# Causal mask of a linear-attention kernel: a DVE product against an ACT copy and a select on Pool

## The chip, the cores and the metric

One Trainium2 chip, one core. The metric is the device time of one execution in microseconds (us); the kernel before takes 953.3 us (median of three runs, 953.12 to 953.48). TensorE is called PE here (its weight loads PEld), VectorE DVE, ScalarE ACT, GpSimd Pool, and SyncE, which issues the transfers, SP.

## What is computed

Gated linear attention over 4 batches x 8 heads x 768 positions of width 48, its output normalised and passed through two feed-forward blocks on 3072 tokens of width 384.

```python
f = 1.0 / (1.0 + np.exp(-f_logit))
for t in range(S):
    state = f[:, :, t, :, None] * state + np.einsum('bhd,bhe->bhde', k[:, :, t], v[:, :, t])
    y[:, :, t] = np.einsum('bhd,bhde->bhe', q[:, :, t], state)
...
rms = np.sqrt(np.mean(x * x, axis=-1, keepdims=True) + 1e-06)
xn = x / rms * rms_g
g = xn @ w_gate
silu = g * (1.0 / (1.0 + np.exp(-g)))
x = silu * (xn @ w_val) @ w_out          # 384 -> 1536 -> 384
...
r = np.maximum(x @ w_in, 0.0)
out = (r * r) @ w_out                    # 384 -> 2048 -> 384
```

## The kernel before

The recurrence is cut into chunks of 128 positions. A unit is one chunk of one batch; there are 24 units, in 6 groups of 4 (512 tokens). For each unit DVE scans the gates (scan_b, scan_a), scales k and q by the decays (mul_k, mul_q), PE forms the 128x128 scores of the 8 heads (`scores`, lines 320 to 329) in two PSUM tiles of 128x512, one for each half of the heads, and the scores are made causal by `mask_part` (lines 331 to 334), called twice for a unit by `masked`. Before the change this is one DVE product of a PSUM tile with a 0/1 tile, written to an SBUF tile `sm`. `attend` (line 355) then multiplies `sm` with v and adds the state's part, giving y; `kv` and `state_add` move the state on; `norm`, `power` (on Pool), `norm2`, `xtrans`, `xhigh`, `xlow` turn y into the transposed input of the feed-forward blocks, split in a high and a low part so that three fast matmuls stand for one in full precision.

The tile `sm` comes from a ring of four buffers (tag "sm", `bufs=4`). The same ring serves `x3o` (`evac_x3_part`, line 806), the three 128x512 tiles in which the first feed-forward block's result of a group is copied out of PSUM by ACT and stored to memory. So the second `sm` tile of the first unit after a group's end waits until a store of `x3o` has landed.

The order on every engine is written out by hand, and each engine works through its own queue in that order:

- Units 0 to 7 and the first group's feed-forward block follow the list FIRST (lines 32 to 48): ma and mb are the two halves of the mask, sc the scores, y attend, kv the state's product, gr, gf the gates, kc the copy of k, no, nr the norm, xh, xl the two splits, ws, wb, wc, wh, wz the conversion of the first block's weights (ws and wh on ACT, wb, wc and wz on DVE), G, V, O the matmuls of one hidden feature block, si, vs, hh, hl the work on their results. G0 is the first of these matmuls.
- Groups 1 to 5 run in steps (`phase1`, line 888). A group has 36 steps, step s = 36 x group + 3 x feature block + 0, 1 or 2. PE does G in the first of three, V in the second, O of the block before in the third; ACT's silu stands in the first, DVE's vs and ACT's hh in the second, DVE's hl in the third. The accumulators g and v have one PSUM bank each, so the next G cannot begin before silu has read the last one. In a step (`segment`, line 794) the planned side work of that step comes first, then silu, vs, hh or hl, then the planned PE work of the attention.
- `plan_unit` (line 670) puts a unit's parts at fixed steps: scores at the end of step s, kcopy and masked in step s + 1, attend at the end of step s + 2, norm in s + 3.
- All other side work is the preparation of the second block's weights, done once, spread over groups 1 to 5: load a raw pair, scale (ACT), three bit operations (DVE), sums and differences (DVE), splits in a high and a low part (ACT and DVE), each split stored to memory; then `open` (line 762), which opens new pools and begins fetching the first 8 of the prepared tiles of 384 KB (`fetch_part`, line 920); then x3, which loads the second block's input (`x3_load`, line 941), and the splits of this input (`x_split`, line 985), an ACT cast and a DVE subtraction for each.
- A planner places these jobs (lines 777 to 784). It goes through them in one order, and a job's step is the first that is not before the step of the job ahead of it and not before its own earliest step (so many steps after a named job: 1 after the last split for `open`, 3 after x3 for the first x split), and in which the job's estimated cost still fits under 2.1 us on each engine it uses, plus an allowance for steps with PE work of the attention. What the units take of each step is entered first from the table COST (lines 687 to 691), the pair (DVE, ACT). The estimates are constants of the code.

After step 215 comes the second feed-forward block (`phase2`, line 1158), which holds no mask.

Of the kernel before, what the change touches and what calls it, by code (L numbers as in the profile page):

```python
# [13 lines left out]
ALU = mybir.AluOpType  # L14
PSUM = bass.MemoryType.PSUM

P = 128
B, H, S, D = 4, 8, 768, 48
C = 128
# [170 lines left out]
def tile_linear_attention_moe(  # L190
# [11 lines left out]
    nc = tc.nc  # L202
# [23 lines left out]
    mask = cp.tile([P, C], F32, name="mask")  # L226
# [29 lines left out]
    U = {}  # L256
# [73 lines left out]

    def mask_part(u, hf):
        sm = ap_.tile([P, 4, C], F32, tag="sm", name=f"sm{u}_{hf}", bufs=4)
        nc.vector.tensor_mul(sm, U[u]["sc", hf], mask.unsqueeze(1).broadcast_to([P, 4, C]))
        U[u]["sm", hf] = sm

    def masked(u):
        mask_part(u, 0)
        mask_part(u, 1)
# [345 lines left out]
    for gi in range(1, NU - 1):  # L684
        for j in range(UG):
            plan_unit((gi + 1) * UG + j, gi * NG + (3 if gi == 1 and j == 0 else (1, 10, 19, 28)[j]))
    COST = dict(
        scan_b=(1.4, 0), keep_end=(0, 0.2), scan_a=(1.2, 0), mul_k=(0.7, 0), mul_q=(0.7, 0), masked=(1.4, 0),
        kcopy=(0, 0.6), gate=(0, 2.2), decay=(0, 1.5), norm=(0, 1.0), norm2=(0, 0.6), state_add=(0.7, 0),
        xhigh=(0, 1.1), xlow=(1.05, 0),  # L690
    )
# [144 lines left out]
    def piece(kind, i):  # L836
        if kind in ("lr", "lk", "lf", "lq", "lv"):
            load_part(kind[1], i)
        elif kind in ("gr", "gf"):
            gate(i) if i >= UG else gate_part(kind[1], i)  # L840
        elif kind in ("ma", "mb"):
            mask_part(i, kind == "mb")
        elif kind in unit_piece:
            unit_piece[kind](i)
        elif kind in pair_piece:
            pair_piece[kind](w1_order[i])
        else:
            step_piece(kind, 0, i)
# [476 lines left out]
```

## Time and profile before

| | us |
|---|---|
| median of three runs | 953.3 |
| the profiled execution | 954.61 |
| its span, first to last instruction | 952.9 |

| engine | busy us | share of the span |
|---|---|---|
| PE | 928.7 | 97% |
| DVE | 629.4 | 66% |
| ACT | 496.3 | 52% |
| Pool | 17.8 | 2% |

How to read it: the table is an average over stages that have different limits. Matmul ends are modelled, so the start of a matmul to the start of the next says more than its busy time. In a timeline row the columns are the start and the duration in us, the engine, the line, the operation, the tile written and those read, the shape and the count; a bracket tells how long the engine stood idle before it and what ended that.

### The profile page before, as it was taken

What the parts mean: (1) busy time and instruction counts of PE and PEld (TensorE: products, weight loads), DVE (VectorE), ACT (ScalarE), POOL (GpSimd) and SP (SyncE); (2) the same over time, 40 slices, a digit from 0 to 9 for tenths busy, and PEclk for the clock granted to TensorE, in tenths of its full rate; (3) what the DMA queues carried; (4) which work ended last, traced back from release to release, by engine and by line L of the source; (5) the groups of instructions that cost most, each with busy time, mean ns of one, the idle gap of its engine ahead of it and who ended that gap; (6) DMA issues with size and microseconds to landing.
All of it is one profiled execution on the core that took longest, in us unless ns stands there. A gap on an engine that the chain in (4) does not pass through costs nothing.

```text
span 952.9 us, 15645 instructions
## 1 busy us (share of the span) xinstructions
PE 928.7 (97%) x6025; PEld 822.2 (86%) x6025; DVE 629.4 (66%) x1147; ACT 496.3 (52%) x1056; POOL 17.8 (2%) x42
## 2 busy tenths in 40 slices
PE   6899999999999999999999999999999999999996
PEld 4687877888888888888888889999999999999996
DVE  7999957655665676666663736756775676666552
ACT  4877555445454555455543425556546554645541
POOL 1000000000000000000000000000000000000000
PEclk6899999999999999999999999999999999999999
DMA  9356342335245154064236057540754075315300
GB/s 336 146 197 223 137 152 88 120 120 194 77 169 183 73 199 160 36 234 155 89 111 248 2 198 256 192 146 12 240 161 129 18 228 164 123 34 182 109 25 28
DMA packets 58081, 135.67 MB, mean 142 GB/s; under 512 B 6800, under 2 KB 25232, under 8 KB 58000
## 3 DMA queue, kind: packets, MB, share of 16 engines
q1 hardware_dynamic: 58000, 134.61, 41.5%
q8 instruction: 49, 0.80, 0.3%
q14 instruction: 32, 0.26, 0.1%
HBM read 108.63 MB, written 25.95 MB: 141 GB/s over the span
## 4 chain that ended last, share of the span: by engine, by line
PE 88%; DVE 4%; DMA 3%; ACT 2%; issue 1%; SPq 0%; POOL 0%; DVEq 0%; ACTq 0%
PE o L644 7%; PE o L643 7%; PE o L642 7%; PE X L1001 7%; PE Y L1001 5%; PE v L642 5%; PE acc L642 5%; PE v L644 5%; PE v L643 5%; PE acc L644 5%; PE acc L643 5%; PE g L642 4%; PE g L643 4%; PE g L644 4%; PE sc L326 2%; PE T L1001 2%
## 5 line engine op out<-in xcount | busy, mean ns | idle before, releaser
L644 PE MATMUL o<-wb,h 128*128 128x384 f32 x384 | 128.6, 335 | 0.0
L643 PE MATMUL o<-wb,h 128*128 128x384 f32 x384 | 128.3, 334 | 0.0
L642 PE MATMUL o<-wb,h 128*128 128x384 f32 x384 | 128.3, 334 | 0.0
L868 DVE TENSOR_TENSOR sg<-v,sg 128x512 f32<-128x512 f32 x72 | 49.6, 689 | 90.9 <-PE v L644 86.4
L871 ACT CAST hh<-sg 128x512 fp32r<-128x512 f32 x72 | 44.4, 617 | 99.4 <-DVE sg L868 99.4
L863 ACT ACTIVATE sg<-g 128x512 f32<-128x512 f32 x72 | 43.0, 597 | 84.7 <-PE g L644 84.6
L1001 PE MATMUL X<-xc,wa 128*128 128x384 f32 x360 | 82.5, 336 | 0.0
L644 PEld LDWEIGHTS o<-wb,h 128*128 128x128 f32 x384 | 72.1, 188 | 0.5
L642 PEld LDWEIGHTS o<-wb,h 128*128 128x128 f32 x384 | 72.1, 188 | 0.0
L643 PEld LDWEIGHTS o<-wb,h 128*128 128x128 f32 x384 | 72.1, 188 | 0.0
L1001 PE MATMUL Y<-xc,wa 128*128 128x384 f32 x300 | 68.3, 335 | 0.0
L1001 PEld LDWEIGHTS X<-xc,wa 128*128 128x128 f32 x360 | 63.8, 188 | 1.8 <-ACT d L1076 1.2
L1080 DVE TENSOR_TENSOR c<-T,c 128x384 f32<-128x384 f32 x40 | 22.3, 558 | 52.7 <-PE T L1001 43.6
L1001 PEld LDWEIGHTS Y<-xc,wa 128*128 128x128 f32 x300 | 53.3, 188 | 0.7 <-DVE c L1080 0.6
L873 DVE TENSOR_TENSOR hl<-sg,hh 128x512 fp32r<-128x512 f32 x72 | 48.9, 681 | 6.0 <-ACT hh L871 5.8
L1031 DVE TENSOR_TENSOR h<-d,h 128x384 fp32r<-128x384 f32 x60 | 32.9, 554 | 26.2 <-ACT h L1030 25.9
L1030 ACT CAST h<-d 128x384 fp32r<-128x384 f32 x60 | 30.2, 511 | 34.4 <-PE o L644 34.4
L1076 ACT COPY d<-X 128x384 f32<-128x384 f32 x40 | 19.2, 480 | 54.7 <-PE X L1001 54.7
L642 PE MATMUL v<-xh,wh_v 128*128 128x512 f32 x108 | 44.2, 410 | 0.0
L642 PE MATMUL g<-xh,wh_g 128*128 128x512 f32 x108 | 43.3, 401 | 0.9 <-ACT xh L443 0.9
L642 PE MATMUL v<-xh,wh_g 128*128 128x512 f32 x108 | 43.7, 405 | 0.0
L642 PE MATMUL acc<-hh,wh_o 128*128 128x512 f32 x108 | 43.2, 400 | 0.0
(181 smaller groups left out, 2243.7 us busy)
## 6 DMA issues: line engine op xcount, KB each, us to landing
wa<-w2d_c SPq DMA_DIRECT2D x100, 384.0 KB, 3.5
raw<-in_w_dram SPq DMA_DIRECT2D x18, 768.0 KB, 4.3
ff<-in_ff_dram SPq DMA_DIRECT2D x20, 516.0 KB, 4.8
qk<-in_qk_dram SPq DMA_DIRECT2D x20, 512.0 KB, 5.7
w2d_c<-ws_c SPq DMA_DIRECT2D x50, 192.0 KB, 2.0
raw_a<-in_w_dram SPq DMA_DIRECT2D x22, 384.0 KB, 3.8
wb<-w2d_b SPq DMA_DIRECT2D x16, 384.0 KB, 3.9
v<-in_vp_dram SPq DMA_DIRECT2D x24, 192.0 KB, 5.7
```

The source lines that it names most:

```text
L642: nc.tensor.matmul(o, lh, rh, start=first, stop=False)
L643: nc.tensor.matmul(o, lh, rl, start=False, stop=False)
L644: nc.tensor.matmul(o, ll, rh, start=False, stop=last)
L863: nc.scalar.activation(dd["s", f], dd["g", f], AF.Silu)
L868: nc.vector.tensor_mul(dd["s", f], dd["v", f], dd["s", f])
L871: nc.scalar.copy(dd["h", f][0], dd["s", f])
L873: nc.vector.tensor_sub(dd["h", f][1], dd["s", f], dd["h", f][0].bitcast(F32))
L1001: nc.tensor.matmul(o, w[a], x[:, b], start=first and n == 0, stop=last and n == 2, skip_group_check=True,)
L1030: nc.scalar.copy(t[:, 0], r)
L1031: later(lambda: nc.vector.tensor_sub(t[:, 1], r, t[:, 0].bitcast(F32)))
L1076: nc.scalar.copy(t, bk[b])
L1080: nc.vector.tensor_add(t, bk[b], t)
```

## The change

`mask_part` no longer multiplies on DVE. ACT copies the score tile from PSUM to `sm`, and Pool then zeroes, in place, the entries on the wrong side of the diagonal, in all four heads of the tile at once. The planner's entry for masked moves from 1.4 us of DVE to 1.2 us of ACT. Nothing else is edited; the places of ma, mb and masked in the orders stay.

```diff
     def mask_part(u, hf):
         sm = ap_.tile([P, 4, C], F32, tag="sm", name=f"sm{u}_{hf}", bufs=4)
-        nc.vector.tensor_mul(sm, U[u]["sc", hf], mask.unsqueeze(1).broadcast_to([P, 4, C]))
+        nc.scalar.copy(sm, U[u]["sc", hf])
+        nc.gpsimd.affine_select(
+            out=sm, in_=sm, compare_op=ALU.is_ge, fill=0.0,
+            base=-(C - 1), pattern=[[0, 4], [1, C]], channel_multiplier=1,
+        )
         U[u]["sm", hf] = sm
...
     COST = dict(
-        scan_b=(1.4, 0), keep_end=(0, 0.2), scan_a=(1.2, 0), mul_k=(0.7, 0), mul_q=(0.7, 0), masked=(1.4, 0),
+        scan_b=(1.4, 0), keep_end=(0, 0.2), scan_a=(1.2, 0), mul_k=(0.7, 0), mul_q=(0.7, 0), masked=(0, 1.2),
         kcopy=(0, 0.6), gate=(0, 2.2), decay=(0, 1.5), norm=(0, 1.0), norm2=(0, 0.6), state_add=(0.7, 0),
```

## Rows read from the trace of the kernel before

**Rows 1.** The page, part 1: busy us, share and instructions of each engine.

```profile
PE 928.7 (97%) x6025; PEld 822.2 (86%) x6025; DVE 629.4 (66%) x1147; ACT 496.3 (52%) x1056; POOL 17.8 (2%) x42
```

**Rows 2.** Busy time by stage; last columns: granted PE clock, DMA share, GB/s.

```profile
24.50:36.30 11.80, 7.34 (x127) 6.05 (x127) 11.66 (x21) 11.39 (x30) 1.98 (x3) 0.93 0.35 137
36.30:145.00 108.70, 105.19 (x729) 83.96 (x731) 96.26 (x146) 71.49 (x137) 2.34 (x4) 0.97 0.50 177
145.00:500.00 355.00, 354.75 (x2576) 292.18 (x2574) 230.94 (x431) 180.56 (x396) 9.20 (x16) 1.00 0.38 133
500.00:545.00 45.00, 45.00 (x200) 37.14 (x200) 22.39 (x42) 16.29 (x32) 0.00 (x0) 1.00 0.37 132
...
519.00:521.00 2.00, 2.00 (x10) 1.66 (x9) 0.12 (x1) 0.43 (x1) 0.00 (x0) 1.00 1.04 409
```

**Rows 3.** Instructions of line 333, ns shortest/median/longest; then what it waited for.

```profile
L333 DVE TENSOR_TENSOR sm<-sc,mask x32: 679/681/692, 145.8 to 482.5; 128x512 f32<-128x512 f32 x32
...
  DMA x3d<-x3o: 10.3, 3
```

**Rows 4.** Timeline of ACT: a PSUM copy of 128x512 and its follower.

```profile
16.46 0.59 ACT L352 COPY ktok<-ktp 128x512 f32<-128x512 f32 x1
16.95 0.63 ACT L289 ACTIVATE r<-r 128x512 f32<-128x512 f32 x1
```

**Rows 5.** Timeline of Pool: a select of 128x128 and a fill of 128x516.

```profile
1.13 0.29 POOL L239 TENSOR_SCALAR_AFFINE_SELECT mask<-mask 128x128 f32<-128x128 f32 x1
1.36 0.53 POOL L243 MEMSET floor<- 128x516 f32 x1
```

**Rows 6.** Timelines of PE, ACT and DVE up to the first feed-forward matmuls.

```profile
21.75 1.09 PE L375 MATMUL y<-v,sm_False 128*64 128x48 f32 x16
...
33.91 1.66 ACT L443 ACTIVATE xh<-xtp,gT 128x128 fp32r<-128x128 f32 x6
...
36.18 2.17 PE L326 MATMUL sc<-qk 64*128 64x128 f32 x16 [2.31 <-issue]
...
39.05 0.78 PE L642 MATMUL g<-xh,wh_g 128*128 128x512 f32 x1
...
42.17 0.40 PE L643 MATMUL g<-xl,wh_g 128*128 128x512 f32 x1
...
36.87 1.64 DVE L450 SCALAR_TENSOR_TENSOR xl<-xtp,gT,xh 128x128 fp32r<-128x128 f32 x6
```

**Rows 7.** Timeline of PE, 88 to 96.5: where it waited for DVE.

```profile
89.82 0.66 PE L345 MATMUL ktp<-ident,qk 128*128 128x128 f32 x4 [0.52 <-DVE qk L304]
...
95.00 1.16 PE L326 MATMUL sc<-qk 64*128 64x128 f32 x16 [0.42 <-DVE qk L307]
```

**Rows 8.** Timelines of PE and DVE at two ends of groups.

```profile
231.77 1.16 PE L326 MATMUL sc<-qk 64*128 64x128 f32 x16
...
237.88 1.09 PE L375 MATMUL y<-v,sm 128*64 128x48 f32 x32
...
329.21 0.69 DVE L333 TENSOR_TENSOR sm<-sc,mask 128x512 f32<-128x512 f32 x1 [4.35 <-DMA x3d<-x3o]
...
329.96 0.67 PE L375 MATMUL y<-v,sm 128*64 128x48 f32 x16 [0.25 <-DVE sm L333]
```

**Rows 9.** Timelines of ACT, SP and PE in group 5: the last split, the fetches, the first x splits.

```profile
505.06 0.95 ACT L578 CAST ws_last<-m_a 128x384 fp32r<-128x384 f32 x2
...
521.61 0.62 ACT L871 CAST hh<-sg 128x512 fp32r<-128x512 f32 x1 [2.18 <-DVE sg L868]
524.13 0.51 ACT L988 CAST xc<-x 128x384 fp32r<-128x384 f32 x1 [1.90 <-DMA x<-x3d]
...
526.16 0.59 ACT L863 ACTIVATE sg<-g 128x512 f32<-128x512 f32 x1
...
509.91 4.76 SPq L927 DMA_DIRECT2D wa<-w2d_c  x8
...
534.89 0.39 PE L642 MATMUL g<-xh,wh_g 128*128 128x512 f32 x1
```

## The prediction, made before the change was run

> **What bounds the kernel now.** The page's first part comes first: PE is busy for 97% of the span, DVE for 66%, ACT for 52%, Pool for 2% [rows 1]. An average over stages doesn't say what an edit is worth, so the next view is the busy time by stage [rows 2]. From 145 to 500 us PE is busy for 354.75 of 355.00 us, and from 500 to 545 for all 45.00: nothing that leaves DVE there can bring anything, and something that makes PE wait costs all it takes. Before 145 us it is different. From 24.5 to 36.3 us DVE (11.66 of 11.80) and ACT (11.39) are both full and PE is not (7.34); from 36.3 to 145 PE has 3.5 us idle, and DVE is at 96.26 of 108.70. So the edit can help only before 145 us, and there it moves work from one full engine to another. Then come the instructions of line 333 [rows 3], the timelines of the start [rows 6, 7] and of two ends of groups [rows 8], and, as the planner's table is edited too, the end of the weight preparation in group 5 [rows 9]. The masks end at 482.5 us [rows 3], so whatever happens in group 5 comes from the table and not from the mask.
>
> **The mask itself.** Removed are 48 DVE products of 0.68 us: 32 of them for units 8 to 23 [rows 3], 16 of the same shape for units 0 to 7. Added are 48 ACT copies from PSUM and 48 selects on Pool. A copy of the same size has 0.59 us, and the next ACT instruction starts 0.49 us after it [rows 4]; I take 0.49 for a copy in a queue. The select is seen at 128x128 only, 0.29 us [rows 5]. Scaled by its columns, a 128x512 select would be 4 x 0.29 = 1.16 us at most; a Pool fill of 128x516 with 0.53 us is the bound below. I take 0.65, near the fill, because a fixed part of the 0.29 doesn't grow with the columns. A half that was ready 0.68 us after its turn on DVE is now ready after 0.59 + 0.65 and two hand-overs of some 0.07 us, 1.4 us, and has to wait for its turn on ACT.
>
> The row of the 128x128 select alone can't tell which of the two bounds holds. The Trainium skill, "GPSIMD Engine Reference", section "Performance versus the Vector engine", gives about 2.6 cycles an element for a two-input operation there and near line rate for one with one input, and advises against Pool for elementwise work. By the slower figure a select would be an estimated 1.1 us and the sum would rise by some 1.5 us, at the start and at the ends of groups.
>
> **The start, to the first feed-forward matmul G0 at 39.05 us.** Eight masks stand here. Off DVE they free 8 x 0.60 = 4.8 us (0.60 is their pitch in a full queue, 0.68 less the overlap), but G0 needs all four units' xh (ACT) and xl (DVE), and ACT is full. Following FIRST: ACT takes mb1 and ma1 only after gf3, which I place to end at 21.1 (no0 ahead of it comes a little earlier than now); the second copy then ends at 22.2, its select, queued behind the first, near 23.1, and y1, which starts at 21.75 now [rows 6], starts some 1.4 us later. Then mb2, ma2, ma3 and mb3 stand in ACT's full stretch ahead of no2: 4 x 0.49 = 2.0 us. Waiting for the select of mb3 before y3 adds some 0.4. ACT's last xh ends at 35.6 now [rows 6] and near 39.3 then; the last xl on DVE follows by 0.9 where DVE now works until 38.5 [rows 6]; G0 starts near 40.5, +1.5 us. Bounds: if ACT's idle moments before 24.5 us took all copies in and DVE alone counted, -2.5; if every copy of the eight fell on the path, 8 x 0.49 = +3.9.
>
> **From G0 to 145 us.** PE waits for DVE at 89.82 and 95.00 us [rows 7]; against the 0.23 us from one matmul's start to the next the two gaps cost 0.67 and 0.58 us. By then six masks (4 and 5, then counting the head start) have left DVE, 2.4 us or more, while PE comes 1.5 us later, so both gaps close: -1.3 us, with some tenths of smaller ones -1.5. The 2.7 us of PE's waiting between 130 and 145 us hang on the group's end (copies of x3o, then xh) and stay. Start and this stretch together: 0, from -4 to +4.
>
> **Units 8 to 23.** From the end of the scores to the first read of sm PE has two steps of other matmuls: 231.77 + 1.16 to 237.88, 4.9 us [rows 8]. In that time ACT does hh's rest, kcopy and the two copies, and Pool the selects: about 3.2 us. That is hidden, and what covers it is 1.7 us. It is gone at three ends of groups, where the second sm buffer waits for the store of x3o (3 waits, 10.3 us together [rows 3]). At 329.21 the product started only then and PE waited for it, to 329.96 [rows 8]; now 1.4 us in place of 0.7 follow the landing: +0.6 us, likewise near 420 us, none at 237. Behind the waiting copy on ACT stands the next silu, which has a spare of a step or two; on Pool only the next unit's `power`. Together +1.1 us, from 0 to +3.
>
> **The planner's table.** This is the largest term. I worked the planner's loop (lines 777 to 784) through with both entries. Until step 92 jobs come up to 7 steps earlier, since DVE has room. Then ACT holds them up: at step 119 kcopy and masked now fill 1.8 of ACT's 2.1, the scale of 0.9 no longer fits and moves on, and the split behind it slides from 120 to 127, past steps full with a norm and a gate. Since jobs keep their order, this adds up: the last splits move from step 182 to 191, `open` from 183 to 192, x3 only from 189 to 192 (PE's freeing of weight tiles held it at 189), and the first x split, three steps after x3, from 192 to 195. Nine steps later for `open`, three for its user. The trace agrees with the plan of before: ws_last stands ahead of the silu of step 183, the first xc ahead of that of 192 [rows 9].
>
> What lies between them is transfers on SP's one queue: the stores of ws_last, then 8 fetches of 384 KB from 509.91 us on, then the x3 loads. The first x cast starts 19.07 us after ws_last (505.06 to 524.13), and already waited 1.90 us for the load [rows 9]. In the new plan ws_last goes behind the hh of step 190: 521.61 + 0.52 = 522.13. The same chain then ends at 522.13 + 19.07 = 541.2. The cast stands ahead of the silu of step 195 in ACT's queue, and between the two lie, as now, 2.03 us (524.13 to 526.16). So this silu starts at 543.2 and ends at 543.8. PE's next G needs the bank that it reads; this G starts at 534.89 now [rows 9]. PE waits for 543.8 - 534.9 = 8.9 us. Bounds: fetches and loads are 8 x 384 KB and 1.2 MB, 4.3 MB in 14.2 us, 300 GB/s; at the 409 GB/s of 519 to 521 us [rows 2] they take 10.5 and the wait is 5.2; with a start 1 us later it is 10.
>
> PE idle for that long loses its clock by all that the start shows: after 2.31 us of waiting, 16 score matmuls took 2.17 us at 36.18, against 1.16 at 95.00, and the rate came back only at 42.17 [rows 6, 7]: 6.0 us at 1.2 GHz in place of 2.4, 3.0 us lost. I add 3.0 (0 to 3.5). The Trainium skill, "TensorE: Matmul & The Clock Gate", section "What's actually happening", has the low clock as the idle default, released by activity; by it too the time after the wait is slow, and the row agrees.
>
> Sum: 0 + 1.1 + 8.9 + 3.0 = +13.0 us. The profiled execution's span is 952.9, its time 954.61, 1.7 more and 1.3 above the median. All terms are differences within the span, so they go on the median: 953.3 + 13.0 = 966.3, taken as 966.
>
> **The rivals.** (a) No stall in group 5: the transfers come much faster or the x split finds its data. For it: the prefetch reaches ahead of ACT's place by itself. Against it: SP can't fetch before ws_last is stored, and the data already came 1.9 us late with 3 + 6 steps between. Time: 953.3 + 1.1 = 954.4. (b) Faster: DVE is what the start hangs on, ACT's idle moments take the copies in, and G0 starts 2.5 us earlier, the two gaps close (-1.5), and (a) holds: 949.3. It decides if ACT in 24.5 to 36.3 us isn't the limit; its 11.39 of 11.80 speaks against it. (c) The masks come late at every unit: if ACT reached the two copies more than 1.7 us later than now at all 16 units, each attend would wait, say 0.7 us: +11 on top, 977. Against it: ACT is busy for only 180.56 of 355 us there [rows 2].
>
> **How the numbers follow.** Forecast, with stall in group 5: 0.83; (a) 0.07; (b) 0.05; (c) 0.05. Within the forecast, the small ends of all terms give 953.3 - 4 + 0 + 5.2 + 0 = 954.5 and the large ends 953.3 + 4 + 3 + 10 + 3.5 = 973.8; all ends at once are unlikely, so the range of 955 to 973 also has room towards (a). Under 0.2% (1.9 us) this kernel's measurement can't tell a change from none: faster 0.06, same 0.07, slower 0.87.
>
> **What would show it.** The right one shows in the profile after as: an idle PE of 6 to 10 us near 535 to 545 us, ended by ACT's silu, behind an xc cast that waits for the DMA of x; a low granted clock behind it; G0 at 40 to 41 us; selects of 0.5 to 1.2 us; no wait of PE at 89 and 95. The forecast is wrong if the first x cast finds its data, if PE waits for sm at ordinary units, or if G0 comes earlier than 39 us.

## The result, and the profile after

The changed kernel takes 966.7 us (median of four runs, 965.58 to 968.12) against 953.2 us (four runs, 953.09 to 953.48): a ratio of 1.0139 with an interval of 1.0126 to 1.0151, so it is slower by 12 to 14 us. The prediction was 966.0 us, slower. Its total held. Its parts held less well, as the section on the prediction shows.

The profiled execution of after took 965.58 us, the fastest of its four, with a span of 963.9 us: 11.0 us more than the span of before, where the medians differ by 13.5; the profiled execution of before (954.61 us) was slower than its four timed ones. The first fence is part 1 of its page, the counterpart of [rows 1].

```profile
PE 929.5 (96%) x6025; PEld 821.3 (85%) x6025; DVE 608.3 (63%) x1099; ACT 519.0 (54%) x1104; POOL 52.8 (5%) x90
```

DVE lost 48 instructions but only 21.1 us of busy time. Forty-eight products of 0.68 us are 32.6 us, so 11.5 us of what DVE should have gained went into its other instructions. ACT took on 22.7 us, Pool 35.0 us, which is 0.73 us for each select.

The same stages as in [rows 2], with group 5 cut at the place of the stall (busy time of PE, PEld, DVE, ACT, Pool; then granted PE clock, DMA share, GB/s):

```profile
24.50:36.30 11.80, 8.12 (x128) 6.70 (x127) 6.34 (x13) 10.45 (x26) 4.99 (x7) 0.87 0.34 132
36.30:145.00 108.70, 103.68 (x722) 82.28 (x721) 93.79 (x138) 75.66 (x147) 9.54 (x13) 0.98 0.48 167
145.00:500.00 355.00, 353.50 (x2572) 290.77 (x2571) 210.17 (x392) 194.95 (x428) 29.70 (x48) 1.00 0.37 127
530.00:545.00 15.00, 8.28 (x37) 6.53 (x35) 2.41 (x4) 1.32 (x3) 0.00 (x0) 0.93 0.82 288
545.00:560.00 15.00, 14.13 (x54) 11.55 (x55) 11.11 (x22) 6.66 (x14) 0.00 (x0) 0.84 0.00 1
```

From 145 to 500 us PE is full, as before: of the 1.50 us that it stands idle, 1.18 lie in the first 3 us, which are the tail of the first group, now later. From 530 to 545 us it is busy for 8.28 of 15.00 us while the DMA share stands at 0.82, and in the next 15 us its clock is 0.84: that is the stall. The timelines of ACT, SP and PE around it answer to [rows 9]:

```profile
525.36 0.92 ACT L582 CAST ws_last<-m_a 128x384 fp32r<-128x384 f32 x2
...
530.95 0.62 ACT L875 CAST hh<-sg 128x512 fp32r<-128x512 f32 x1 [2.18 <-DVE sg L872]
543.20 0.51 ACT L992 CAST xc<-x 128x384 fp32r<-128x384 f32 x1 [11.63 <-DMA x<-x3d]
544.81 0.51 ACT L992 CAST xc<-xs 128x384 fp32r<-128x384 f32 x1 [1.09 <-DVE xs L981]
545.22 0.59 ACT L867 ACTIVATE sg<-g 128x512 f32<-128x512 f32 x1
...
526.90 0.89 SPq L585 DMA_DIRECT2D w2d_b<-ws_last  x2
529.56 4.02 SPq L931 DMA_DIRECT2D wa<-w2d_c  x8
533.68 5.45 SPq L951 DMA_DIRECT2D x<-x3d  x6
...
537.89 0.39 PE L648 MATMUL acc<-hh,wl_o 128*128 128x512 f32 x1
545.87 0.80 PE L646 MATMUL g<-xh,wh_g 128*128 128x512 f32 x1 [7.59 <-ACT sg L867]
...
549.86 0.40 PE L646 MATMUL v<-xh,wh_g 128*128 128x512 f32 x1
```

Read it from the end. PE waits 7.59 us for the silu of step 195 at 545.22. The silu stands behind two xc casts, and the first of these waited 11.63 us for its data. The data came late because SP issues the loads of x (533.68) behind the 8 fetches of wa (529.56), and those behind the stores of ws_last, which is now split behind the hh of step 190 rather than in step 183.

The rest of the time is lost at the start. These are PE's rows there that answer to [rows 6, 7], with the new waits between them:

```profile
22.74 1.09 PE L379 MATMUL y<-v,sm_False 128*64 128x48 f32 x16 [1.91 <-POOL sm_False L334]
33.79 0.67 PE L379 MATMUL y<-v,sm_True 128*64 128x48 f32 x16 [1.25 <-POOL sm_True L334]
40.61 0.76 PE L646 MATMUL g<-xh,wh_g 128*128 128x512 f32 x1
46.81 0.50 PE L646 MATMUL g<-xh,wh_o 128*128 128x512 f32 x1 [1.13 <-ACT sg L867]
92.03 0.66 PE L349 MATMUL ktp<-ident,qk 128*128 128x128 f32 x4 [0.22 <-DVE qk L304]
97.20 1.16 PE L326 MATMUL sc<-qk 64*128 64x128 f32 x16 [0.42 <-DVE qk L307]
108.30 0.67 PE L379 MATMUL y<-v,sm_False 128*64 128x48 f32 x16 [0.64 <-POOL sm_False L334]
```

How far PE has been put back at a matmul is its start here less the start of the same matmul before. The figures are 1.56 us at G0 (40.61 - 39.05), 2.21 us at 92.03, 3.02 us at 108.30, 3.2 us ahead of the stall, 10.98 us at its end (545.87 - 534.89) and 12.92 us when the full clock is back.

These starts hold more than the change. The granted clock from 12 to 24.5 us was 0.50 in the profiled execution of before and 0.71 in that of after. Three other profiled kernels of the next section (e1, e4 and e8) have the same start as after, up to G0. In e1 and e8, where that clock was 0.50 as in before, G0 stands at 41.37 and 41.56 us, 2.3 and 2.5 us later than before. In e4 it was 0.64, and G0 stands at 40.73.

At the last matmul the put-back is 12.6 us. The end of the span then comes 1.6 us sooner behind that matmul than it did before (6.65 against 8.26 us). What follows there is the same two evacuations and the same three stores, so this is a spread of the last stores from one execution to the next.

### The profile page after: what moved, and what is told of

It is laid out like the page before. It is cut to its first block, busy times and chain, and to the rows that moved or that the text cites. A ratio compares the mean times of both kernels' runs of the same rounds, so it can differ in the third digit from the quotient of the medians.

```text
span 963.9 us, 15730 instructions
## 1 busy us (share of the span) xinstructions
PE 929.5 (96%) x6025; PEld 821.3 (85%) x6025; DVE 608.3 (63%) x1099; ACT 519.0 (54%) x1104; POOL 52.8 (5%) x90
## 4 chain that ended last, share of the span: by engine, by line
PE 86%; DVE 5%; ACT 4%; DMA 2%; issue 2%; POOL 1%; SPq 0%; DVEq 0%; ACTq 0%
PE o L648 7%; PE o L646 7%; PE o L647 7%; PE X L1005 7%; PE Y L1005 5%; PE v L646 5%; PE acc L646 5%; PE v L648 4%; PE v L647 4%; PE g L646 4%; PE g L647 4%; PE acc L647 4%; PE acc L648 4%; PE g L648 4%; PE sc L326 2%; PE y L379 2%
## 5 line engine op out<-in xcount | busy, mean ns | idle before, releaser
L646 PE MATMUL g<-xh,wh_o 128*128 128x512 f32 x108 | 42.6, 394 | 1.1 <-ACT sg L867 1.1
```

The source lines that it names most:

```text
L646: nc.tensor.matmul(o, lh, rh, start=first, stop=False)
```

## The experiments

Each was timed together with the kernel before on the same chip, and each time the median of that was 954.5 us. The loss in us is the ratio's excess of 954.5 us, which can differ by some tenths from the difference of the medians. Put-back means the same as above, against the profiled execution of before. Diffs are against before, or against after where the sentence says so.

**The two halves of the change.** The first run has the new mask and the old table entry, the second the old mask and the new entry.

```diff
 e1:  mask_part as in after;  masked=(1.4, 0)
 e2:  nc.vector.tensor_mul(sm, ...) as before;  masked=(0, 1.2)
```

> The mask goes to ACT and Pool as in the change, the planner's table keeps masked=(1.4, 0), so every job stays at its old step. Theory (the table moves open to step 192 and PE then waits for the x load): no long wait of PE in group 5; what is left is the start and the first group, which in the trace after had put PE back by 3.0 us at 105 us and 3.2 at 421 us: 953.2 + 3.2 = 956.4, 955 to 958. Rival (ACT and Pool are the cost, the table is not): 965 to 967.

Measured: 959.2 us, ratio 1.0048 (1.0031 to 1.0064), 4.6 us, more than was expected. Group 5 has no stall, as the stage from 500 to 545 us shows:

```profile
500.00:545.00 45.00, 45.00 (x201) 37.14 (x200) 23.45 (x42) 16.34 (x31) 0.00 (x0) 1.00 0.36 132
```

> The mask stays the DVE product, the planner's table alone is edited to masked=(0, 1.2). Theory: open at step 192, x split at 195, PE waits some 8 to 9 us for the silu of step 195 near 532 to 541 us and then runs for about 5 us at the low clock: 953.2 + 8.5 + 2 = 963.7, 961 to 966; some tenths more if DVE is now overbooked in masked steps. Rival: 953 to 954.

Measured: 962.5 us, ratio 1.0080 (1.0064 to 1.0097), 7.6 us. ACT and PE in group 5:

```profile
521.77 0.92 ACT L578 CAST ws_last<-m_a 128x384 fp32r<-128x384 f32 x2
539.93 0.51 ACT L988 CAST xc<-x 128x384 fp32r<-128x384 f32 x1 [11.95 <-DMA x<-x3d]
...
542.60 0.79 PE L642 MATMUL g<-xh,wh_g 128*128 128x512 f32 x1 [7.91 <-ACT sg L863]
```

The stall is here whole, without a single instruction of the change in the kernel: a constant that costs no time of its own makes 0.80% of the 1.39%. The two halves add up to 1.28%, which is the whole within the intervals. The mask alone costs 0.48%, some four times what the prediction gave it.

**What in group 5 makes the stall.** Two runs keep the whole change. One lets the x splits come at least 8 steps after x3, not 3; the other puts the job that loads x ahead of the job that begins the 8 fetches.

```diff
 e4 (against after)
-            at_least = ((None, last0 + 3 * (f + 1) + 3), (("x3",), 3))
+            at_least = ((None, last0 + 3 * (f + 1) + 3), (("x3",), 8))
 e8 (against after)
-        job(("open",), open_late, after=((("plain", na[1]), 1), (None, last0 + 2)))
         job(("x3",), lambda: (x3_tiles(), x3_load(0)), after=((None, last0 + 9),))
+        job(("open",), open_late, after=((("plain", na[1]), 1), (None, last0 + 2)))
```

> The change whole, but the first x split is planned 8 steps after x3 in place of 3, step 200 instead of 195; nothing is left out. Theory: the load has landed before ACT comes to the cast, the wait of PE and the low clock behind it are gone: 966.7 - 9.7 = 957, 955 to 959. Rival (the time is lost because open itself comes late, or by ACT's load): 964 to 967.

Measured: 957.5 us, ratio 1.0031 (1.0019 to 1.0042). The stage of the stall, then SP and ACT:

```profile
530.00:545.00 15.00, 15.00 (x68) 12.40 (x67) 4.13 (x7) 3.47 (x6) 0.00 (x0) 1.00 0.82 290
...
534.22 5.28 SPq L951 DMA_DIRECT2D x<-x3d  x6
...
543.26 0.62 ACT L875 CAST hh<-sg 128x512 fp32r<-128x512 f32 x1 [2.18 <-DVE sg L872]
543.79 0.51 ACT L992 CAST xc<-x 128x384 fp32r<-128x384 f32 x1
```

> The change whole, with two lines of the plan swapped: the x3 loads are issued ahead of open and its 8 fetches, x3 at step 191, open at 192, the first x split at 194. Nothing is left out. Theory (the x loads stand behind 3.1 MB of fetches in SP's queue): the loads land within 5 us of the stores of ws_last, the first cast waits less than 3 us, PE does not wait: 3 to 4 us over the kernel before, as with the x splits planned later. Rival (open's own late start costs): 9 us or more over it.

Measured: 958.5 us, ratio 1.0038 (1.0025 to 1.0050). The stage of the stall, then SP and ACT:

```profile
530.00:545.00 15.00, 15.00 (x68) 12.43 (x67) 8.14 (x15) 5.29 (x12) 0.00 (x0) 1.00 0.86 299
...
529.36 2.81 SPq L951 DMA_DIRECT2D x<-x3d  x6
532.27 4.53 SPq L931 DMA_DIRECT2D wa<-w2d_c  x8
...
534.83 0.51 ACT L992 CAST xc<-x 128x384 fp32r<-128x384 f32 x1 [1.78 <-DMA x<-x3d]
```

Either edit takes the stall away, PE being busy for all 15 us, and what is left agrees within the intervals with what the mask alone costs. In e4 the transfers are issued at nearly the same times as in after, and the cast, asked for later, waits for nothing. In e8 the cast follows the same hh on ACT as in after. Its loads are issued 4.3 us earlier, its wait ends 5.5 us after the first of them and not 9.5, and ACT comes to it 1.5 us later: 11.63 us of waiting become 1.78. So the cause is the order in SP's one queue together with the short distance between loading x and using it.

**Which units the mask costs.** Three runs have the old table and the new mask in one stage only.

```diff
     def mask_part(u, hf):
+        if u >= 2 * UG:          # e3;  e6: u < UG;  e7: UG <= u < 2 * UG
             nc.scalar.copy(sm, U[u]["sc", hf])
             nc.gpsimd.affine_select(out=sm, in_=sm, ...)
+        else:
+            nc.vector.tensor_mul(sm, U[u]["sc", hf], mask...)
```

> Old table; units 0 to 7 keep the DVE product, units 8 to 23 have the ACT copy and the select. Theory (steady units are hidden, the ends of groups cost some tenths): 953.2 + 0.3 = 953.5, 952.9 to 954.5. Rival (masks on ACT come late at every unit): 16 x 0.2 to 0.7 = 956 to 964. The difference to the run with the mask alone is the price of the start.

Measured: 954.9 us, ratio 1.0004 (0.9994 to 1.0014). PE is full from 145 to 500 us:

```profile
145.00:500.00 355.00, 355.00 (x2567) 292.36 (x2566) 216.90 (x399) 195.99 (x428) 30.61 (x48) 1.00 0.38 132
```

> Old table; only units 0 to 3 have the ACT copy and the select. Theory (the wait of y1 and ACT's full stretch set G0, which came 1.6 us later in the trace after): 1 to 2.5 us over the kernel before. Rival (DVE is what the start hangs on, it gains 4.8 us): 1 to 3 us under it.

Measured: 957.8 us, ratio 1.0035 (1.0023 to 1.0046), above the 1 to 2.5 us expected. G0 is put back 3.04 us (42.09), at a granted clock of 0.50 from 12 to 24.5 us as before:

```profile
23.74 1.10 PE L382 MATMUL y<-v,sm_False 128*64 128x48 f32 x16 [1.52 <-POOL sm_False L335]
...
42.09 0.78 PE L649 MATMUL g<-xh,wh_g 128*128 128x512 f32 x1
```

> Old table; only units 4 to 7 have the ACT copy and the select. The step of the prediction for 39 to 145 us (relieved DVE closes the gaps at 89.82 and 95.00): 1 to 1.5 us under the kernel before. Theory after the profile (the first silu waits behind two more copies on ACT, the select of unit 6 is stretched, the gaps stay half open): 0.5 to 2 us over it.

Measured: 956.0 us, ratio 1.0016 (1.0007 to 1.0026). Put-back goes from -0.30 us at G0 to +1.0 at 106 us; the largest single new wait is this one, of PE, behind this select on Pool:

```profile
106.30 0.67 PE L382 MATMUL y<-v,sm_False 128*64 128x48 f32 x16 [0.62 <-POOL sm_False L335]
...
104.80 1.45 POOL L335 TENSOR_SCALAR_AFFINE_SELECT sm_False<-sm_False 128x512 f32<-128x512 f32 x1 [0.85 <-POOL sm_True L335]
```

In us the three cost 0.4, 3.3 and 1.5, together 5.2, against 4.6 for the mask in all units. Thirty-two of the 48 masks cost nothing that can be measured. The other 16, all before 126 us, cost everything. For units 4 to 7 the prediction's step, which had them bring a gain of 1 to 1.5 us, is refuted.

**Why the start gets later.** Three runs take the new mask apart. The first keeps the kernel before whole and adds 48 selects, which read `sm` and write a tile that nobody reads. The second is e6 with the masks earlier in FIRST: mb1 and ma1 right behind sc1, mb2 and ma2 behind xt1. The third is e6 without the selects, so units 0 to 3 keep the scores above the diagonal.

```diff
 e5 (against before)
         nc.vector.tensor_mul(sm, U[u]["sc", hf], mask...)
+        sx = ap_.tile([P, 4, C], F32, tag="sx", name=f"sx{u}_{hf}", bufs=1)
+        nc.gpsimd.affine_select(out=sx, in_=sm, ...)
 e9 (against e6), in FIRST
-... kc1 sc1 sa2 mq2 ... gf3 mb1 kv1 ma1 mk2 y1 ... xt1 sc3 gr4 wl2 xl0 kt2 mb2 ma2 ma3 y2
+... kc1 sc1 mb1 ma1 sa2 mq2 ... gf3 kv1 mk2 y1 ... xt1 mb2 ma2 sc3 gr4 wl2 xl0 kt2 ma3 y2
 e10 (against e6)
-            nc.gpsimd.affine_select(out=sm, in_=sm, ...)
```

> The kernel before, with the DVE product and the old table, plus 48 selects on Pool that read each sm tile and write a scratch tile that nobody reads: Pool works as in the change, and nothing waits for it. Theory (Pool and DVE slow each other down, as the profile after shows DVE only 21.1 us less busy for 48 products of 0.68 us = 32.7 us taken away): DVE busy time goes up from 629.4 to about 637 to 643, selects that run beside full DVE take 0.8 to 1.6 us instead of 0.64, and as DVE is full up to 126 us the end comes 1 to 4 us later. Rival (the longer DVE times after had another cause): DVE at 629 to 631, time within 0.1%.

Measured: 957.7 us, ratio 1.0034 (1.0020 to 1.0048). Part 1 of its page, and two of its DVE instructions that run beside the selects at 21.11 and 22.19 us:

```profile
PE 927.8 (97%) x6025; PEld 820.5 (86%) x6025; DVE 641.4 (67%) x1147; ACT 496.1 (52%) x1056; POOL 58.5 (6%) x90
...
21.54 1.39 DVE L538 TENSOR_TENSOR wl_g<-m,wh_g 128x768 fp32r<-128x768 f32 x1
22.86 1.65 DVE L293 TENSOR_TENSOR_SCAN r<-r,floor 128x516 f32<-128x516 f32 x1
```

DVE runs the same 1147 instructions as before and is busy for 12.0 us more (641.4 against 629.4 in [rows 1]). PE waits for none of these selects, and yet the kernel is 3.2 us slower. G0 is put back 0.93 us and the matmul of 89.82 us by 2.1; after 126 us nothing is added. That goes with a slowed DVE: PE's waits for DVE up to 126 us add up to 7.1 us, against 5.3 before. The selects also stand ahead of `power` in Pool's queue, but PE's waits for xn, which hangs on `power`, went only from 1.6 to 1.8 us. These are sums of one execution each, and no run takes the two apart.

> As the run with the new mask in units 0 to 3 (1.0035 of the kernel before), but five places in the list FIRST moved: mb1 and ma1 stand right behind sc1 (ahead of gr3, no0 and gf3 on ACT), mb2 and ma2 ahead of gr4. Theory (the places of the copies in ACT's queue set the start): y1 and y2 no longer wait for a select, G0 comes 1 to 2 us earlier, 1.0013 to 1.0025 of the kernel before. Rival (the slowing of DVE by Pool, or ACT's sum, sets it, wherever the copies stand): 1.003 to 1.004.

Measured: 956.2 us, ratio 1.0016 (1.0007 to 1.0025). Rows of PE:

```profile
20.39 1.10 PE L382 MATMUL y<-v,sm_False 128*64 128x48 f32 x16 [0.42 <-POOL sm_False L335]
...
32.80 0.67 PE L382 MATMUL y<-v,sm_True 128*64 128x48 f32 x16 [1.82 <-POOL sm_True L335]
...
39.93 0.77 PE L649 MATMUL g<-xh,wh_g 128*128 128x512 f32 x1
```

y1 starts 3.35 us earlier than in e6, and G0 2.16 us earlier. That is about half of e6's loss: it came from where the copies stand in ACT's order. The wait for mb3's select, which wasn't moved, stays (1.82 us), and y1 still waits 0.42 us for a select, where no wait was expected.

> As the run with the new mask in units 0 to 3, but without the eight selects: the ACT copies alone stand in the place of the DVE products, and the scores above the diagonal of these units stay in (this part of the computation is left out). Theory (half of the 3.3 us are the wait of y1, y2 and y3 for a select and the slowing of DVE by Pool, half the copies in ACT's full stretch): 1.0010 to 1.0025 of the kernel before. Rival (the copies on ACT are all of it): 1.003 to 1.004. Second rival (the selects are all of it): 0.998 to 1.000, DVE being relieved by 4.8 us.

Measured: 955.2 us, ratio 1.0008 (0.9999 to 1.0017). Rows of PE:

```profile
20.19 0.88 PE L393 MATMUL kv<-v,ktok 128*48 128x48 f32 x16 [2.95 <-ACT sm_True L334]
...
31.48 0.67 PE L378 MATMUL y<-v,sm_True 128*64 128x48 f32 x16 [1.45 <-ACT sm_True L334]
...
39.29 0.77 PE L645 MATMUL g<-xh,wh_g 128*128 128x512 f32 x1
```

The copies on ACT alone cost 0.8 us (-0.1 to 1.6) of the 3.3, less than the half expected, though PE does wait for them. The selects therefore cost some 2.5 us at the start. e9 takes 1.8 and e10 2.5 of the 3.3 us away, more than the whole together, so the parts overlap, and an exact split between the selects' own delay, their slowing of DVE, and the copies' place stays open. From execution to execution the starts also differ by about 1 us where no edit touches them. In e3, in which everything up to 126 us is as before, the granted clock from 12 to 24.5 us was 0.86 in place of 0.50, G0 stands at 37.97 us, 1.08 us earlier, and the span ends at 952.2 us, 0.7 us ahead of before. So put-backs of about 1 us in the start aren't settled by one profile, and the medians above carry the argument.

None of these versions is faster than the kernel before.

## Why the prediction was right, step by step

**What bounds the kernel.** The reading of [rows 2] held. From 145 to 500 us nothing was won or lost. The loss fell before 126 us and on group 5, the two places named.

**The prices.** The select was taken at 0.65 us from bounds of 0.53 and 1.16. All 48, by tile (ns shortest/median/longest):

```profile
L334 POOL TENSOR_SCALAR_AFFINE_SELECT sm<-sm x32: 634/637/1350, 149.6 to 486.1; 128x512 f32<-128x512 f32 x32
L334 POOL TENSOR_SCALAR_AFFINE_SELECT sm_False<-sm_False x8: 637/746/1557, 12.4 to 125.4; 128x512 f32<-128x512 f32 x8
L334 POOL TENSOR_SCALAR_AFFINE_SELECT sm_True<-sm_True x8: 637/658/1040, 13.4 to 124.5; 128x512 f32<-128x512 f32 x8
```

The select takes 0.64 us when alone, near the bound from the fill. But it reaches 1.56 us in units 0 to 7, and the prediction had no term for that. The copy was 0.59 us, as taken.

**The start, predicted +1.5 us.** The profile shows 1.56 us at G0, and the way there is the predicted one: the second copy of unit 1 ends at 20.7 us (22.2 predicted), its select at 22.7 (23.1), y1 starts at 22.74. The agreement to a tenth is luck: at the clock of before the same start is 2.3 to 2.5 us later (e1, e8). The 8 masks of units 0 to 3 alone cost 3.3 us by their runs, inside the bounds given (-2.5 to +3.9) but twice the value taken. Waiting for the select of mb3 ahead of y3 was put at 0.4 us and is 1.25.

**From G0 to 145 us, predicted -1.5 us: this is the step that failed.** The profile shows +1.5 (from 1.56 to 3.02 us of put-back), and e7 measures +1.5 for units 4 to 7. The step said that DVE, relieved of six masks, would close the gaps at 89.82 and 95.00, and that no wait there would show it right. They are still there, at 92.03 (0.22 us in place of 0.52) and at 97.20 (0.42, as before).

DVE did lose four masks between G0 and the first of these gaps, an estimated 2.4 us at the 0.60 of the prediction, and yet it reaches the `qk` that PE waits for at 91.31 us where it reached it at 89.10, as late as PE itself. The head start from the first eight masks was gone before that, since DVE waits for xh (0.46 us at 38.82). Two things took most of the rest. Three bit operations that ran beside a select (40.98, 45.01 and 80.62 us) took 1.43, 1.36 and 1.27 us in place of 0.96, together 1.2 us. Another 0.9 us went into DVE's own waits, 1.4 us against 0.5 before in the same stretch: 0.23, 0.43 and 0.34 us for ACT, which now does the copies, and 0.41 for PE. So the step had wrong that DVE alone sets the gaps, and that a mask taken from DVE frees what it cost there. That selects lengthen what DVE runs beside them is what e5 measures; the part of ACT's waits is read from one trace.

From 24.5 to 36.3 us DVE has room (6.34 of 11.80 us busy, 11.66 before), but there PE waits for the selects themselves.

The rows are a bit operation up to 126 us, grouped (total us, mean ns of one), in the trace of before and in that of after, and from after's timelines two scans, a wait of DVE for ACT and a select:

```profile
L482 DVE SCALAR_TENSOR_TENSOR m<-raw,m 128x768 int32<-128x768 int32 x18 | 17.2, 958 | 0.6
```
```profile
L486 DVE SCALAR_TENSOR_TENSOR m<-raw,m 128x768 int32<-128x768 int32 x18 | 19.1, 1064 | 0.6
...
17.24 1.23 DVE L301 TENSOR_TENSOR_SCAN f<-f,seed 128x516 f32<-128x516 f32 x1
20.59 1.67 DVE L293 TENSOR_TENSOR_SCAN r<-r,floor 128x516 f32<-128x516 f32 x1
46.79 0.69 DVE L872 TENSOR_TENSOR sg<-v,sg 128x512 f32<-128x512 f32 x1 [0.43 <-ACT sg L867]
...
21.13 1.56 POOL L334 TENSOR_SCALAR_AFFINE_SELECT sm_False<-sm_False 128x512 f32<-128x512 f32 x1
```

The same scan shape takes 1.23 us alone and 1.67 us beside selects (20.29 and 21.13 us). In before, all 16 scans up to 126 us have a mean of 1.23 us, also from 12 to 24.5 us, where the DMA share is the same 1.04, so the transfers aren't the cause. Three new waits came on top: 1.13 us for the first silu, which stands behind a copy of the mask on ACT (44.28) and the table load behind that (1.28 us, as before), 0.48 us at 80.30 for ACT, and 0.64 us at 108.30 for a select that was stretched to 1.44 us.

The Trainium skill, "GPSIMD Engine Reference", section "Key points", says that Pool shares its interfaces to SBUF with VectorE and contends with DVE instructions in a 2-port mode or with two SBUF inputs. The slowed scan (r and floor) and the bit operation (raw and m) both read two, and the rows agree. The prediction weighed this page's figure for the speed of an instruction and passed over this sentence, which bears on the step that failed.

**Units 8 to 23, predicted +1.1 us.** The profile shows 0.2, e3 0.4 (-0.6 to 1.3). The cover of 1.7 us was there. Of the three ends of groups, the wait at 329.96 [rows 8] disappeared, since PE comes some 3 us later, and one appeared at 423.93:

```profile
423.93 0.67 PE L379 MATMUL y<-v,sm 128*64 128x48 f32 x16 [0.32 <-POOL sm L334]
```

**The planner's table.** The steps were right: splits that slide until step 191, the first xc after the hh of step 193 and ahead of the silu of step 195, PE idle behind it. Two sizes were off. From ws_last to the xc it took 17.84 us (525.36 to 543.20) rather than 19.07, and PE lost 7.75 us (537.89 to 545.87, less the pitch of 0.23) rather than 8.9. The low clock then cost 1.9 us rather than 3.0: nine matmuls from 545.87 to 549.86, 3.99 us where they need 2.05. The start, from which the 3.0 was taken, had stayed at the lower rate for 6.0 us, and here it was 4.0. In e2 the same pair appears, 7.91 us of waiting and the low rate behind it.

**Why the sum held.** In the profile the terms came out 1.1, 1.1 and 0.9 us lower (wait, clock, units 8 to 23) and 3.0 us higher (G0 to 145), which leaves -0.1: the put-back is 12.9 us when the full clock is back, and the sum was 13.0. By the runs the split is plainer: the mask was put at +1.1 us and costs 4.6, the table at +11.9 and costs 7.6. The sign, the place and the mechanism of the larger half were understood; that the total came within 1 us is in part the luck of errors that cancel.

**The rivals.** (a), no stall, is what e1 shows at 4.6 us, not the 1.1 that it was priced at. (b), faster, falls: even with no selects in units 0 to 3 (e10) G0 comes at 39.29 us, not earlier than the 39.05 of before. (c), late masks at every unit, falls by e3.

## What to carry to other kernels

A cost table that only plans is part of the schedule: a corrected entry moved a prefetch by nine steps and its user by three, and that cost more than the instructions that the entry describes, so compare the planned distance of each load and its use before and after such an edit. Work moved from DVE to Pool isn't off DVE as long as both run at once: price it by the DVE time that remains, not by the instructions removed. And where one queue carries several transfers, put the one with the nearest user first; here the swap of two lines took away a wait of 7.6 us.

## What was not expected of the hardware

Pool and DVE slow each other here. A 128x512 select of 0.64 us takes up to 1.56 us beside DVE, a 128x516 scan of 1.23 us then 1.67, and two 128x768 operations of 0.95 us, wl_g in e5 and m at 105.49 us in after, took 1.39 and 1.27. Forty-eight selects that nobody reads cost DVE 12.0 us of busy time, 0.25 us each. The rows read like turns: in after a select runs from 44.92 to 45.56 us, and the bit operation that starts at 45.01 ends at 46.37, 0.81 us behind it, where it takes 0.96 alone. That the two take turns is a reading of such rows; no run tests it.
